# Half products for w_res in the last three blocks, and a changed order of rows, in an attention and gated feed-forward kernel

## The chip, the cores and the metric

The kernel runs on one core of one Trainium2 chip. The metric is the device time of one execution in microseconds. A core has TensorE (PE in the profile; its weight loads are PEld), VectorE (DVE), ScalarE (ACT), GpSimd (POOL) and SyncE (SP), which run side by side, each through its own queue of instructions in order, and wait for each other through semaphores. TensorE writes to PSUM, which has eight banks; VectorE and ScalarE read and write PSUM and SBUF, GpSimd SBUF alone.

## What is computed

Eight batches, eight heads, 576 tokens, head size 64. Without a softmax, attention is two products and a normalisation; its result, seen as 4608 tokens of 512 channels, goes through a gated feed-forward layer with a gated residual:

```python
kv  = einsum('bhsd,bhse->bhde', k, v)
out = einsum('bhsd,bhde->bhse', q, kv)
x   = out / sqrt(mean(out * out) + 1e-6) * g_norm     # as [4608, 512]
ffn = (gelu(x @ w_gate) * (x @ w_val)) @ w_out        # 512 -> 1536 -> 512
y   = x + sigmoid(x @ w_res) * ffn                    # w_res is 512 x 512
```

## The kernel before, in words

**Blocks.** The tokens are worked in nine blocks of 512 (blk 0 to B, B = 8): the first 512 tokens of each batch are a block, and the remaining 64 of each batch make up the last one. TensorE does the matmuls of a block in this order: gate and value products, w_res product, w_out product. The attention of a later batch is laid between them, two blocks ahead. Matmuls have f16 operands of 128x128 (stationary) by 256 or 512 columns and gather in f32 in PSUM.

**Seven products for eight.** From block 2 on most products are made in the manner of Strassen and Winograd: both operands are split into quadrants, sums and differences of quadrants are made beforehand, and seven half-sized products take the place of eight. `gv_group` (L708) does so for four column tiles of w_gate (g) and w_val (v): each half product is four matmuls of 256 columns, named in the order lists (L703) as `1g 1v Eg 5g Ev 5v dg 6g ...`. A digit is a product; `E` is a copy by ScalarE of product 1 out of bank A into bank E, on which product 2 adds; `d` is a copy by ScalarE of product 5 into SBUF; `F` and `c` are sums A + d on VectorE, F back into a PSUM bank, c into SBUF; `g11` to `g22` are the gelu of a quarter on ScalarE; `h11` to `h22` multiply it by the value quarter into the tile `hid`, h22 on GpSimd, the rest on VectorE. Products 6, 7 and 4 add onto the same bank A in turn, so 6 waits for the copies of 1, 7 for the F sum, and 4 for the c sum. A block of three groups takes bank A from two banks by turns, and exchanges the banks of E and F from group to group (`banks_of`, L1263).

**Sums.** `token_sums` (L688) makes four sums of quadrants of a block's transposed tokens, used for w_gate and w_val; `weight_sums` (L662) those of the weights, once. For w_out, `wo_sums` (L465) makes those of the weights, and `s_begin`, `s_rest`, `s_last` (L470 to L482) those of `hid` (s2; s0 and s1; s3), all on VectorE.

**w_res.** `m_res` (L412) does the w_res product in full: for each of four rows of 128 tokens, four matmuls of 512 columns into a bank of its own, then a tanh on ScalarE into `th_all`; 16 matmuls of 512 columns in a block. `m_sigmoid` (L427) makes the sigmoid from the tanh, later.

**w_out.** `out_by_products` (L497) returns four steps: `res(0)`, `res(1)`, `first_two` and `others`. `first_two` makes s3, product wA with its copy to wE, product wD with its copy wd, and the sigmoids; `others` makes the other five products of 12 matmuls each, the sums wF and c22, and the multiplies `pf` by the sigmoid into `osb` (`res_all`). Then `fin` adds x on GpSimd, and `store` issues a store on SP. `out_last` (L577) does this for block 8 in finer steps: u = sigmoid times wd plus x, on GpSimd, spares a later addition, and four pairs of stores go out, on SP's and ScalarE's queues.

**Other work laid between.** `a_t` (L330) writes normalised attention rows t out of PSUM (VectorE, t(0) to t(3), and t(4) for the remaining tokens), `a_x` (L353) multiplies them by g_norm (VectorE), `a_norm` is a chain of twelve small steps on GpSimd. The order of all of this is written out by hand: `at` puts work behind a slot of a block, `at_word(blk, i, word, ...)` behind a word of a group's order list, and `aside_out(blk, key, ...)` ahead of a step of `first_two` and `others` ("D", "F", "00", "22", "01", "11").

Of the kernel before, what the change touches and what calls it, by code (L numbers as in the profile page):

```python
# [18 lines left out]
def kernel(  # L19
# [15 lines left out]
    nc = tc.nc  # L35
# [439 lines left out]
    def s_rest(blk):  # L475
# [2 lines left out]
        sub(nc.vector, s_[0], a_of(blk, 2, 1), a_of(blk, 2, 2), ALU.add)  # L478
        sub(nc.vector, s_[1], s_[0], a_of(blk, 1, 1))

    def s_last(blk):
        sub(nc.vector, hid_sums[3], a_of(blk, 1, 2), hid_sums[1])  # L482

    def prod(ps, a, b, start, es=(0, 1)):

        for e in es:
            for f in range(NFH):
# [6 lines left out]
                    skip_group_check=True,  # L494
                )

    def out_by_products(blk, later, banks, amid):  # L497
        w = {}
        s_ = hid_sums

        def aside(ahead_of):
            for f in amid.get(ahead_of, ()):
                f()

        def res(jj):
            for j in (2 * jj, 2 * jj + 1):
                m_res(blk, j, banks[j])

        def first_two():
            for n in ("D", "E", "F", "A"):  # L510
                w[n] = pmoe.tile([P, 2, CH], FP32, name="w" + n, bank=banks[n])
            w["d"] = attnp.tile([P, 2, CH], FP32, tag="sq", bufs=3, name="wd")
            s_last(blk)
            prod(w["A"], a_of(blk, 1, 1), b_of(1, 1), True)
            nc.scalar.copy(out=w["E"], in_=w["A"])
            aside("D")
            prod(w["D"], s_[0], wo_t[:, 0], True)
            nc.scalar.copy(out=w["d"], in_=w["D"])
            aside("gates")
            for j in range(NJ):  # L520
                m_sigmoid(j)

        def part(jj):
            return slice(None), slice(2 * jj[0], 2 * jj[0] + 2), slice(jj[1] * CH, (jj[1] + 1) * CH)

        def pf(jj, src, eng=nc.vector):
            eng.tensor_tensor(out=res_all[part(jj)], in0=th_all[part(jj)], in1=src, op=ALU.mult)  # L527

        def fin(jj):
            of = part(jj)  # L530
            nc.gpsimd.tensor_tensor(out=res_all[of], in0=res_all[of], in1=t_t[blk][of], op=ALU.add)  # L531

        def store(jj):
            dst = out[blk * S : blk * S + M0, :].rearrange("(p j) c -> p j c", j=NJ)
            js = slice(2 * jj, 2 * jj + 2)
            nc.sync.dma_start(out=dst[:, js, :], in_=res_all[:, js, :])

        def others():


            prod(w["A"], s_[1], wo_t[:, 1], False)
            aside("F")
            sub(nc.vector, w["F"], w["A"], w["d"], ALU.add)
            aside("00")
            prod(w["E"], a_of(blk, 1, 2), b_of(2, 1), False)
            pf((0, 0), w["E"])
            aside("22")
            prod(w["A"], s_[2], wo_t[:, 2], False)
            c22 = res_all[part((1, 1))]
            sub(nc.vector, c22, w["A"], w["d"], ALU.add)  # L550
            aside("01")
            prod(w["F"], s_[3], b_of(2, 2), False)
            pf((0, 1), w["F"])
            aside("11")
            prod(w["A"], a_of(blk, 2, 2), wo_t[:, 3], False)
            if whole(blk + 1):
                pf((1, 1), c22, nc.gpsimd)
                pf((1, 0), w["A"])
            else:
                pf((1, 1), c22)  # L560
                pf((1, 0), w["A"])
            if later:
                return
            for i in (1, 0):
                fin((i, i))
                fin((i, 1 - i))
                store(i)

        if later:
            x = [lambda j=j: a_x(blk, j) for j in range(NJ)]  # L570
            at_word(blk + 1, 0, "1v", *x[0:2], lambda: fin((0, 0)), lambda: fin((0, 1)), lambda: store(0))
            at_word(blk + 1, 0, "Fv", x[2])
            at_word(blk + 1, 0, "cv", x[3])
            at_word(blk + 1, 0, "h22", lambda: fin((1, 0)), lambda: fin((1, 1)), lambda: store(1))
        return [lambda: res(0), lambda: res(1), first_two, others]

    def out_last(blk, banks):  # L577

        s_ = hid_sums

        def bank(n, i):
            return pmoe.tile([P, n, CH], FP32, name="w", bank=i)

        def part(j, n, ch):
            return slice(None), slice(j, j + n), slice(ch * CH, (ch + 1) * CH)

        def gated(j, n, ch, src):
            of = part(j, n, ch)
            nc.vector.tensor_tensor(out=res_all[of], in0=th_all[of], in1=src, op=ALU.mult)

        def plus(j, n, ch, eng):
            of = part(j, n, ch)
            eng.tensor_tensor(out=res_all[of], in0=res_all[of], in1=t_t[blk][of], op=ALU.add)

        def store(j, n, c0, c1):
            for e, queue in enumerate((nc.sync, nc.scalar)):
                dst = out.rearrange("(j e s) c -> e s j c", e=2, s=S)[e, M0:S, j : j + n, c0:c1]
                queue.dma_start(out=dst, in_=res_all[e * R : (e + 1) * R, j : j + n, c0:c1])

        def run():  # L600
            wa = [bank(1, banks["A"][e]) for e in range(2)]
            wd, we, wf = [bank(2, banks[n]) for n in "DEF"]
            d = attnp.tile([P, 2, CH], FP32, tag="sq", bufs=3, name="wd")
            u = attnp.tile([P, 2, CH], FP32, tag="sq", bufs=3, name="u")
            one = (slice(0, 1), slice(1, 2))
            s_last(blk)
            for e in range(2):
                prod(wa[e], a_of(blk, 1, 1), b_of(1, 1), True, (e,))
            for j in (2, 3):
                m_sigmoid(j)  # L610
            for e in range(2):
                nc.scalar.copy(out=we[:, one[e], :], in_=wa[e])
            prod(wd, s_[0], wo_t[:, 0], True)
            nc.scalar.copy(out=d, in_=wd)
            for j in (0, 1):
                m_sigmoid(j)
            for e in range(2):
                prod(wa[e], s_[1], wo_t[:, 1], False, (e,))
                sub(nc.vector, wf[:, one[e], :], wa[e], d[:, one[e], :], ALU.add)
            sub(nc.gpsimd, u, th_all[part(2, 2, 1)], d, ALU.mult)  # L620
            sub(nc.gpsimd, u, u, t_t[blk][part(2, 2, 1)], ALU.add)
            prod(we, a_of(blk, 1, 2), b_of(2, 1), False)
            gated(0, 2, 0, we)
            plus(0, 2, 0, nc.gpsimd)
            store(0, 2, 0, CH)
            prod(wf, s_[3], b_of(2, 2), False)
            gated(0, 2, 1, wf)
            plus(0, 2, 1, nc.gpsimd)
            store(0, 2, CH, C)
            for e in range(2):  # L630
                prod(wa[e], s_[2], wo_t[:, 2], False, (e,))
                gated(2 + e, 1, 1, wa[e])
            of = part(2, 2, 1)
            sub(nc.vector, res_all[of], res_all[of], u, ALU.add)
            store(2, 2, CH, C)
            for e in range(2):
                prod(wa[e], a_of(blk, 2, 2), wo_t[:, 3], False, (e,))
                gated(2 + e, 1, 0, wa[e])
                plus(2 + e, 1, 0, nc.vector)
            store(2, 2, 0, CH)  # L640

        return [lambda: [m_res(blk, j, banks[j]) for j in range(NJ)], run]

    LAST = (B - 1, B)
    GF = 4
# [533 lines left out]
    def plan_attn_ahead(b):  # L1179
# [40 lines left out]
        if whole(m + 1):  # L1220
            t = [lambda j=j: a_t(b, j) for j in range(NJ + 1)]
            x = [lambda j=j: a_x(b, j) for j in range(NJ + 1)]
            for i, word, fs in (
                (0, "Fv", t[2:3]),
                (0, "cv", t[3:4]),
                (1, "1v", x[0:1]),
                (1, "Fv", t[4:5]),
                (1, "cv", x[1:2]),
                (2, "1v", [*x[2:4], lambda: d_xT(b, 0, NJ)]),
                (2, "Fv", [x[4], lambda: d_xT(b, NJ, NJ + 1)]),  # L1230
            ):
                at_word(m + 1, i, word, *fs)
# [21 lines left out]
    for blk in GROUPS:  # L1254
        t = token_sums(blk, nc.vector)
        if blk == 2:
            at(blk - 1, NF + 3, *t)
            continue
        for key, f in zip(("00", "00", "22", "01") if whole(blk) else ("00", "22", "01", "11"), t):
            aside_out(blk - 1, key, f)  # L1260
    out_at = {}

    def banks_of(blk):  # L1263
# [18 lines left out]
        if blk not in LAST:  # L1282
            if len(groups) % 2:
                ga0, ga1, va0, va1, ge_, gf, ve, vf = ga1, ga0, va1, va0, gf, ge_, vf, ve
            out_at[blk] = {0: ge_, 1: ga1, 2: ve, 3: ge_, "A": va1, "D": ga1, "E": ve, "F": ge_}
            att_at[blk] = [gf, vf, ga0, va0]
            pmoe.turn = [out_at[blk][n] for n in "DEFA"]
        else:
            out_at[blk] = {0: ga1, 1: va1, 2: ge_, 3: ve}
# [9 lines left out]
    for blk in range(B + 1):  # L1299
# [21 lines left out]
        else:  # L1321
            slots = [lambda f=f: m_gval(blk, f) for f in range(NF)]
            groups = GROUPS.get(blk, ())
            if groups:
                n = NF - GF * len(groups)
                slots[n:] = [None] * (NF - n)
                ends = []
                at_word(blk, len(groups) - 1, "h12", lambda: s_begin(blk))

                def group(i, blk=blk, ends=ends):  # L1330
                    if i == 0:
# [20 lines left out]
                plan.setdefault(NFH + 2, []).insert(0, lambda: s_begin(blk))  # L1352

            def products(blk=blk, outs=outs):
                s_rest(blk)
                if blk not in GROUPS:
                    out_at[blk] = banks_behind()
                if blk < B:
# [57 lines left out]
```

## Time and profile before

| | |
|---|---|
| Runs of the kernel before | 325.02, 325.13, 324.98, 324.41 us; median 325.0 |
| The profiled execution | 325.02 us; its span, first to last instruction, 323.2 us |
| TensorE (PE) busy | 315.0 us, 97% of the span, 2936 matmuls |
| VectorE (DVE) busy | 263.9 us, 82%, 482 instructions |
| ScalarE (ACT) busy | 201.3 us, 62%, 367 instructions |
| GpSimd (POOL) busy | 145.0 us, 45%, 212 instructions |
| TensorE's mean granted clock | 0.996 of full speed |
| w_res products of blocks 6, 7, 8 start at | 243.04, 274.00, 304.96 us |

How to read it: times in the timelines count from the span's start. A timeline row has the start, the time from the first start to the last end, the engine, the line, the operation, output and inputs with shapes, and how many instructions are merged; in brackets stand the idle time ahead of it and the engine that a program inferred to have ended it. Matmuls overlap: four of 256 columns show 0.60 us from the start of the first to the end of the last, and the next four start 0.437 us after them. Spans on GpSimd are rough. Names in rows are those of the tiles: `Ag` is bank A of the gate product, `wA` that of the w_out product, `rps` the w_res product, `ts` token sums, `hid_s` the sums s0 to s3, `osb` the output rows.

### The profile page before, as it was taken

The page shows a single profiled execution, that of the slowest core. Times are in us where ns is not written, and L with a number is a line of the kernel's source. Part 1 is how long each engine was busy: PE and PEld are TensorE (multiplying, and loading weights), DVE is VectorE, ACT ScalarE, POOL GpSimd, SP SyncE. Part 2 cuts the span into 40 slices and gives each one's busy share as a digit, 9 for nine tenths or more (in the row PEclk, how much of TensorE's full clock was granted, in tenths as well). Part 3 has the DMA queues.
Part 4 walks back from the last instruction along what each step waited for, and adds up shares of the span by engine and source line. Part 5 has one row for each costly group of instructions (what it writes and reads, how often), then busy time and mean ns, then how long its engine had stood idle before and what let it go on. Part 6 is the DMA issues. An engine that isn't in the chain of part 4 may idle for free.

```text
span 323.2 us, 7458 instructions
## 1 busy us (share of the span) xinstructions
PE 315.0 (97%) x2936; PEld 236.4 (73%) x2936; DVE 263.9 (82%) x482; ACT 201.3 (62%) x367; POOL 145.0 (45%) x212
## 2 busy tenths in 40 slices
PE   8989999999999999999999999999999999999993
PEld 3544755444867878886888688868887888788782
DVE  5788879789799887998799879998896777677754
ACT  3673685465727784868487848684766467636760
POOL 2793251573712678337843784117511242042232
PEclk9999999999999999999999999999999999999998
DMA  7999999699995599389938893720322030002004
GB/s 255 324 204 204 194 206 177 164 179 134 156 138 98 180 131 99 133 162 121 112 132 157 109 128 131 118 50 2 130 43 40 2 130 4 0 32 102 0 2 130
DMA packets 76693, 38.89 MB, mean 120 GB/s; under 512 B 42098, under 2 KB 74354, under 8 KB 76658
## 3 DMA queue, kind: packets, MB, share of 16 engines
q0 software_dynamic: 38752, 17.17, 42.1%
q1 hardware_dynamic: 37328, 20.71, 24.9%
q10 hardware_dynamic: 578, 0.52, 0.5%
q8 instruction: 23, 0.38, 0.5%
q14 instruction: 12, 0.10, 0.1%
HBM read 38.80 MB, written 9.44 MB: 149 GB/s over the span
## 4 chain that ended last, share of the span: by engine, by line
PE 96%; DVE 3%; issue 0%; DVEq 0%
PE Av L737 12%; PE Ag L737 12%; PE wA L488 11%; PE rps L415 10%; PE gps L395 6%; PE vps L395 6%; PE Fv L737 6%; PE Fg L737 6%; PE fps L432 3%; PE wD L488 3%; PE Ev L737 3%; PE wF L488 3%; PE wE L488 3%; PE Eg L737 3%; PE w L488 2%; PE idle L902 2%
## 5 line engine op out<-in xcount | busy, mean ns | idle before, releaser
L774 POOL TENSOR_TENSOR hid<-ge,c 128x512 f16<-128x512 f16 x21 | 24.4, 1163 | 69.5 <-ACT ge L768 69.5
L531 POOL TENSOR_TENSOR osb<-osb,t 128x512 f32<-128x512 f32 x28 | 31.6, 1158 | 36.1 <-DVE osb L527 25.1
L488 PEld LDWEIGHTS <-hid_s 128*128 128x128 f16 x384 | 37.5, 98 | 4.4
L737 PEld LDWEIGHTS <-wsv 128*128 128x128 f16 x336 | 32.7, 97 | 4.5
L737 PEld LDWEIGHTS <-wsg 128*128 128x128 f16 x336 | 32.7, 98 | 3.9
L415 PE MATMUL rps<-wr,xT 128*128 128x512 f16 x144 | 33.4, 380 | 0.0
L488 PEld LDWEIGHTS <-hid 128*128 128x128 f16 x288 | 28.1, 98 | 5.1
L747 ACT COPY Eg<-Ag 128x512 f32<-128x512 f32 x21 | 12.2, 582 | 25.9 <-PE Ag L737 25.9
L758 DVE TENSOR_TENSOR Fg<-Ag,d 128x512 f32<-128x512 f32 x21 | 14.6, 697 | 16.4 <-ACT d L751 11.1
L383 ACT ACTIVATE ge<-gps 128x512 f16<-128x512 f32 x24 | 14.1, 597 | 21.3 <-PE gps L395 21.2
L737 PEld LDWEIGHTS <-wg 128*128 128x128 f16 x252 | 24.3, 98 | 3.7 <-issue 0.4
L737 PEld LDWEIGHTS <-wv 128*128 128x128 f16 x252 | 24.6, 97 | 3.3 <-issue 0.2
L424 ACT ACTIVATE th<-rps 128x512 f32<-128x512 f32 x36 | 21.1, 594 | 8.1 <-PE rps L415 8.0
L737 PE MATMUL Ag<-ts,wsg 128*128 128x256 f16 x168 | 25.2, 273 | 0.0
L737 PE MATMUL Av<-ts,wsv 128*128 128x256 f16 x168 | 25.2, 272 | 0.0
L254 DVE TENSOR_REDUCE ss<-sq 128x8 f32<-128x512 f32 x32 | 20.1, 679 | 5.7 <-ACT sq L249 5.7
L415 PEld LDWEIGHTS <-xT 128*128 128x128 f16 x144 | 13.5, 98 | 14.2
L395 PE MATMUL gps<-xT,wg 128*128 128x512 f16 x88 | 22.6, 379 | 0.0
L395 PE MATMUL vps<-xT,wv 128*128 128x512 f16 x88 | 22.6, 379 | 0.0
L488 PE MATMUL wA<-wo_ts,hid_s 128*128 128x256 f16 x168 | 20.6, 273 | 0.0
L384 DVE TENSOR_TENSOR hid<-ge,vps 128x512 f16<-128x512 f16 x24 | 16.3, 685 | 4.8 <-PE vps L395 4.0
L429 ACT ACTIVATE th<-th 128x512 f32<-128x512 f32 x36 | 20.1, 641 | 0.0
(188 smaller groups left out, 766.4 us busy)
## 6 DMA issues: line engine op xcount, KB each, us to landing
out_dram<-osb SPq DMA_DIRECT2D x14, 512.0 KB, 2.6
qraw<-in_q_dram POOLq DMA_DIRECT2D x7, 512.0 KB, 6.9
k<-in_k_dram POOLq DMA_DIRECT2D x7, 512.0 KB, 9.4
v<-in_v_dram POOLq DMA_DIRECT2D x7, 512.0 KB, 11.2
wg<-in_moe_w_gate_dram POOLq DMA_DIRECT2D x2, 512.0 KB, 8.1
wv<-in_moe_w_val_dram POOLq DMA_DIRECT2D x2, 512.0 KB, 8.5
wo<-in_moe_w_out_dram POOLq DMA_DIRECT2D x2, 512.0 KB, 13.9
out_dram<-osb SPq DMA_DIRECT2D x4, 256.0 KB, 4.6
```

Source lines behind the costliest of these rows:

```text
L254: nc.vector.tensor_reduce(out=out_, in_=sqs.pop((b, i)), op=ALU.add, axis=mybir.AxisListType.X)
L383: nc.scalar.activation(out=ge, in_=gps, func=AF.Gelu)
L384: nc.vector.tensor_tensor(out=hids[blk][:, f, :], in0=ge, in1=vps, op=ALU.mult)
L395: nc.tensor.matmul(ps[:, j0 * P : j1 * P], lhsT=w[:, cc, :], rhs=xT_t[blk][:, j0:j1, cc, :], start=(cc == 0 and j0 == 0), stop=(cc == NP - ...
L415: nc.tensor.matmul(rps, lhsT=xT_t[blk][:, j, cc, :], rhs=wr16[:, cc, :], start=(cc == 0), stop=(cc == NP - 1),)
L424: nc.scalar.activation(out=th, in_=rps, func=AF.Tanh, scale=0.5)
L429: nc.scalar.activation(out=th, in_=th, func=AF.Copy, scale=0.5, bias=0.5)
L488: nc.tensor.matmul(ps[:, e - es[0], :], lhsT=a[:, f, e * P : (e + 1) * P], rhs=b[:, f, :], start=(start and e == es[0] and f == 0), stop=( ...
L531: nc.gpsimd.tensor_tensor(out=res_all[of], in0=res_all[of], in1=t_t[blk][of], op=ALU.add)
L737: nc.tensor.matmul(out_[:, r, :], lhsT=lhsT, rhs=rhs, start=(first and r == 0 and c == 0), stop=(c == 1), skip_group_check=True,)
L758: nc.vector.tensor_tensor(out=dst, in0=ps["A", u], in1=sb["d", u], op=ALU.add)
L774: eng.tensor_tensor(out=dst, in0=ge[q], in1=source(q, "v"), op=ALU.mult)
```

## The change

For blocks 6, 7 and 8 (`res_in_halves`), the w_res product is made in seven half products too (`res_halves`): 28 matmuls of 256 columns. Its seven products stand in the order `1 sE 5 sd 6 +F 2 tE 7 +c 3 tF 4 tc tA`, where `s` are copies on ScalarE, `+` sums on VectorE, and `t` the four tanh. Between them are laid the two halves of w_out's product wA (after `sd` and `+F`), the first half of product wD (after `tF`), the sums s0 to s3 one by one (`s_sum`), and the copy to wE. `s_begin`, `s_rest` and `s_last` are left out in these blocks. The wd copy and all four sigmoids follow the last half of wD; in block 8 two of the sigmoids stood ahead of it before. In block 6 the banks of w_res and w_out are given anew.

Four sums of w_res quadrants (`wr_sums`) are made once on VectorE: two in block 5's w_out part, ahead of wD and ahead of the wF sum, two in the last group of block 6, behind `Fv` (ahead of the a_x there) and behind `cv`.

In the first group of blocks 3 to 6, t(2) moves from behind `Fv` to behind `1v`, t(3) from behind `cv` to behind `Fv`. In block 2, two additions `fin` and a store move from behind `1v` to behind `cv` in the recorded order.

```diff
+    def s_sum(blk, i):
+        s_ = hid_sums
+        if i == 0:
+            sub(nc.vector, s_[0], a_of(blk, 2, 1), a_of(blk, 2, 2), ALU.add)
+        elif i == 1:
+            sub(nc.vector, s_[1], s_[0], a_of(blk, 1, 1))
+        elif i == 2:
+            sub(nc.vector, s_[2], a_of(blk, 1, 1), a_of(blk, 2, 1))
+        else:
+            sub(nc.vector, s_[3], a_of(blk, 1, 2), s_[1])
...
+    def res_halves(blk, banks, amid):
...
+        def product(p):
+            n = {1: "A", 2: "E", 3: "F", 4: "A", 5: "F", 6: "A", 7: "A"}[p]
+            first = p in (1, 5)
+            out_ = bank(n) if first else ps[n]
+            s_of = {3: 3, 5: 0, 6: 1, 7: 2}
+            t_of = {4: 3, 5: 0, 6: 1, 7: 2}
...
+            w_ = wr_s[0][:, s_of[p]] if p in s_of else wr_quadrant(*quad[p])
+            x_ = x_sums[blk][:, t_of[p]] if p in t_of else x_quadrant(blk, *xq[p])
+            for e in range(2):
+                for cc in range(2):
+                    nc.tensor.matmul(out_[:, e, :], lhsT=x_[:, e, cc, :], rhs=w_[:, cc, :], ...
...
+        for word in "1 sE 5 sd 6 +F 2 tE 7 +c 3 tF 4 tc tA".split():
+            n = word[-1]
+            if word.isdigit():
+                product(int(word))
+            elif word == "sE":
+                nc.scalar.copy(out=bank("E"), in_=ps["A"])
+            elif word == "sd":
+                sb["d"] = attnp.tile([P, 2, CH], FP32, tag="sq", bufs=3, name="rd")
+                nc.scalar.copy(out=sb["d"], in_=ps["F"])
+            elif word[0] == "+":
+                if n == "c":
+                    sb["c"] = attnp.tile([P, 2, CH], FP32, tag="o32", bufs=3, name="rc")
+                nc.vector.tensor_tensor(out=bank("F") if n == "F" else sb["c"], in0=ps["A"], in1=sb["d"], op=ALU.add)
+            else:
+                tanh(n)
+            for f in amid.get(word, ()):
+                f()
...
+        def with_res():
+            res_halves(blk, dict(zip("AFE", (banks[j] for j in range(3)))), {
+                "sd": [tiles_of_w, lambda: half("A", 0, a_of(blk, 1, 1), b_of(1, 1)), lambda: s_sum(blk, 0)],
+                "+F": [lambda: half("A", 1, a_of(blk, 1, 1), b_of(1, 1)), lambda: s_sum(blk, 1),
+                       lambda: nc.scalar.copy(out=w["E"], in_=w["A"])],
+                "+c": [lambda: s_sum(blk, 2), lambda: s_sum(blk, 3)],
+                "tF": [lambda: half_d(0)],
+            })
+            half_d(1)
+            nc.scalar.copy(out=w["d"], in_=w["D"])
+            for j in range(NJ):
+                m_sigmoid(j)
...
-            at_word(blk + 1, 0, "1v", *x[0:2], lambda: fin((0, 0)), lambda: fin((0, 1)), lambda: store(0))
+            at_word(blk + 1, 0, "1v", *x[0:2])
             at_word(blk + 1, 0, "Fv", x[2])
-            at_word(blk + 1, 0, "cv", x[3])
+            at_word(blk + 1, 0, "cv", x[3], lambda: fin((0, 0)), lambda: fin((0, 1)), lambda: store(0))
...
+        if res_in_halves(blk):
+            return [with_res, lambda: None, lambda: None, others]
         return [lambda: res(0), lambda: res(1), first_two, others]
...
+            half_d(1)
             nc.scalar.copy(out=d, in_=wd)
-            for j in (0, 1):
+            for j in (2, 3, 0, 1):
                 m_sigmoid(j)
...
-                (0, "Fv", t[2:3]),
-                (0, "cv", t[3:4]),
+                (0, "1v", t[2:3]),
+                (0, "Fv", t[3:4]),
...
+    wr_ = wr_sums(nc.vector)
+    aside_out(LAST[0] - 2, "D", wr_[0])
+    aside_out(LAST[0] - 2, "F", wr_[1])
+    for word, f in (("Fv", wr_[2]), ("cv", wr_[3])):
+        at_word(LAST[0] - 1, 2, word, f)
...
             att_at[blk] = [gf, vf, ga0, va0]
+            if res_in_halves(blk):
+                out_at[blk] = {0: ga0, 1: va0, 2: ve, "A": gf, "D": vf, "E": ge_, "F": ga1}
+                att_at[blk] = [ga0, va0, ve, va1]
```

## The prediction

> **What bounds the kernel now.** I read first the page's engine table and its chain that ended last, then the chain in order of time, then each engine's timeline around the edits. The chain is TensorE nearly alone:
>
> ```profile
> PE 96%; DVE 3%; issue 0%; DVEq 0%
> ```
>
> So time is won by fewer matmul columns, or where TensorE waits for a helper; work elsewhere costs only when it makes TensorE or the last store late. In the chain in order of time, block 6 shows both prices (start, us, engine, output, line, count):
>
> ```profile
> 243.20 3.45 PE rps L415 x16
> 246.65 1.31 PE wA L488 x12
> ```
>
> A 512-column matmul takes 3.45/16 = 0.216 us, a 256-column one 1.31/12 = 0.109 us, half: nothing is lost by cutting.
>
> TensorE's timeline gives the waits: a product of four such matmuls starts 0.437 us after the last one where nothing is late, its result is there 0.60 after its start. Block 3, second group:
>
> ```profile
> 133.45 0.60 PE L737 MATMUL Ag<-ts,wsg 128*128 128x256 f16 x4
> 133.99 0.60 PE L737 MATMUL Av<-ts,wsv 128*128 128x256 f16 x4
> ...
> 135.30 0.60 PE L737 MATMUL Ag<-ts,wsg 128*128 128x256 f16 x4
> 135.83 0.60 PE L737 MATMUL Av<-ts,wsv 128*128 128x256 f16 x4
> ```
>
> Both gaps are 0.10 too long (one more of 0.04 stands before 137.61): 0.24 in this group. Its rows on VectorE and ScalarE say why:
>
> ```profile
> 131.13 0.68 DVE L341 TENSOR_TENSOR t<-op,ny 128x512 f16<-128x512 f32 x1
> 131.73 0.68 DVE L774 TENSOR_TENSOR hid<-ge,Ev 128x512 f16<-128x512 f16 x1
> 132.32 0.68 DVE L774 TENSOR_TENSOR hid<-ge,Fv 128x512 f16<-128x512 f16 x1
> ```
> ```profile
> 132.44 0.59 ACT L747 COPY Eg<-Ag 128x512 f32<-128x512 f32 x1
> 133.37 0.57 ACT L747 COPY Ev<-Av 128x512 f32<-128x512 f32 x1 [0.34 <-PE Fg L737]
> ```
>
> The copy to Ev writes the bank that hid<-ge,Fv has read until 133.00 (the releaser named is a guess); it ends 133.94, and the matmuls of 133.99 follow. Block 5 repeats this (Fv read until 198.92, Ev at 199.28, gaps 0.10, 0.09, 0.04). In blocks 4 and 6 Ev starts 0.09 after the read, and the group has no gap.
>
> **The change part by part.** Latencies from the same rows: TensorE's end to VectorE 0.11 (250.58 to 250.69), to ScalarE 0.04; VectorE to TensorE 0.06 (240.80 to 240.86), to ScalarE 0.09.
>
> *Order of t, blocks 3 to 6.* The first t goes ahead of the Fg sum, into 1.20 us in which VectorE sat idle (126.94 to 128.13): free. The second takes the first one's slot, so the hid multiplies come 0.60 earlier; hid<-ge,Fv ends 132.40, Ev follows Eg at 132.96 and ends 133.53, before 133.89. The a_x behind them ends 134.06 as before, since GpSimd's multiply (132.62 to 133.78) holds it. Fg then waits for the matmuls only (133.45 + 0.60 + 0.11 = 134.16, was 134.48), and the gaps of 0.10, 0.09 and 0.04 close. Two blocks: **-0.47**. Ends: 0, if something else than the read held Ev, and -0.48.
>
> *Block 2.* The additions fin((0, 0)) and fin((0, 1)) move in the text, but in the built programs every engine has the same instructions in the same order in block 2, and the additions wait for the same second a_x. The wait they cause stays:
>
> ```profile
> 100.78 2.27 POOL L531 TENSOR_TENSOR osb<-osb,t 128x512 f32<-128x512 f32 x2 [10.61 <-DVE t L355]
> ```
> ```profile
> 99.28 1.42 DVE L355 TENSOR_TENSOR t<-t,g 128x512 f16<-128x512 f16 x4
> ...
> 102.06 1.27 DVE L355 TENSOR_TENSOR t<-t,g 128x512 f16<-128x512 f16 x1
> ```
>
> One a_x took 1.27 instead of 0.41: it could end only 0.28 after GpSimd's addition did. TensorE lost 0.34 + 0.16 there, and will again: **0**.
>
> *Sums of w_res.* Four operations of 128x512 f16, 0.42 us each as the token sums. The first, in block 5, falls into 0.60 us of idle VectorE ahead of 218.09. The second starts 219.29, before the wF sum (219.62, becomes 219.63), and holds GpSimd's first norm step (219.46) some 0.10; the next step waits for a token sum until about 220.5 anyway, which takes the delay up. **0**; at most +0.24, the whole of it, because norm, t (224.10), osb (225.31), Ev (226.07 to 226.64) and the matmuls at 226.77 follow each other closely.
>
> The other two stand in block 6's last group:
>
> ```profile
> 240.72 0.41 DVE L355 TENSOR_TENSOR t<-t,g 128x512 f16<-128x512 f16 x1
> 241.06 0.67 DVE L758 TENSOR_TENSOR c<-Ag,d 128x512 f32<-128x512 f32 x1
> 241.66 0.67 DVE L758 TENSOR_TENSOR c<-Av,d 128x512 f32<-128x512 f32 x1
> ```
>
> One more operation at 240.72 (0.34 apart) moves the c sums to 241.40 and 242.00. 4g (242.16) needs the first at 242.07 + 0.06: in time. 4v (242.60) needs the second at 242.67 + 0.06 = 242.73: **+0.13**. The other sum, behind the c sums, and the later gelu move hid<-ge,Fv from 242.91 to 243.53, end 244.21.
>
> *Half products of w_res.* Per block 28 x 0.109 = 3.06 instead of 3.45: -0.39 each. Waits that come new, counted from the first half product, block 7 (274.00 in the old clock): product 1 at 0, 5 at 0.44, half of wA 0.87, 6 at 1.53, half of wA 1.97, 2 at 2.62, 7 at 3.06, 3 at 3.50, half of wD 3.94, 4 at 4.59, half of wD 5.03, done 5.68 (6.07 before). Product 6 needs the seed of E: 0.64 to 1.22, in time. Product 7 needs the F sum: 6 is there 2.13, sum 2.24 to 2.93 (0.69 as the Fg sum), + 0.06 = 2.99, **0.07 ahead**. On VectorE stand before it hid<-ge,Av (0.56 to 1.24) and s0 (1.16 to 2.11, which needs GpSimd's multiply, 0.69). s1 follows (2.84 to 3.80), then c, 3.77 to 4.46; product 4 needs 4.52, again 0.07 ahead. s2 and s3 end by 6.2; s3's product starts 9.6. The gates: wd copy 5.88, four sigmoids until 8.55; osb<-th,wE waited for them before too and goes with them. Block 7: **-0.39**; ends -0.39 and +0.03 (both loops 0.28 longer, the spread between Ev's 0.09 and 0.36).
>
> Block 6: the E seed goes to the bank that hid<-ge,Fv reads until 244.21, so it runs 244.30 to 244.88; product 6 would start 243.17 + 1.53 = 244.70 and starts 244.94: +0.24. -0.39 + 0.13 + 0.24 = **-0.02**; ends -0.39 and +0.26 (seed 0.28 later).
>
> Block 8: matmuls -0.39 too, but the tail hangs on GpSimd. The sigmoids of rows 2, 3 ran before the wd copy; now all follow it.
>
> ```profile
> 311.90 1.27 POOL L463 TENSOR_TENSOR u<-th,wd 128x512 f32<-128x512 f32 x1 [6.25 <-ACT wd L614]
> 313.25 1.16 POOL L463 TENSOR_TENSOR u<-u,t 128x512 f32<-128x512 f32 x1
> 314.68 2.41 POOL L593 TENSOR_TENSOR osb<-osb,t 128x512 f32<-128x512 f32 x2 [0.28 <-DVE osb L589]
> ```
> ```profile
> 317.00 0.69 DVE L463 TENSOR_TENSOR osb<-osb,u 128x512 f32<-128x512 f32 x1
> ```
>
> The wd copy starts 310.84, the second sigmoid behind it ends 312.45: u starts 312.5 (was 311.90), and the four GpSimd steps end 317.26 (was 317.09). VectorE's osb<-osb,u is ready 0.40 earlier, 316.60, and has two inputs in SBUF like the a_x of block 2. If GpSimd holds it likewise, until 317.13, it ends 317.81 (was 317.69), and the last addition and the last store are 0.12 late: **+0.12**. If not, the last addition ends 318.88 (was 319.28), but the second and third stores now leave 0.2 later, the transfers of the fourth queue behind them, and -0.19 is left. I take +0.12: the a_x row is the nearest, and osb is no less an SBUF operand for being f32. Ends: -0.39 and +0.20.
>
> Sum: -0.47 + 0 + 0 - 0.02 - 0.39 + 0.12 = -0.76. The profiled execution took 325.02 us (span 323.2 and 1.8 around it; the median of four is 325.0): **324.3**. All low ends: -0.48 - 3 x 0.39 = -1.65, 323.4. All high ends: 0 + 0.24 + 0.03 + 0.26 + 0.20 = +0.73, 325.8.
>
> Two rules of the Trainium skill bear on this. The page "TensorE: Matmul & The Clock Gate" (Back-to-back issue gap) gives some 131 ns for 512 columns and 81 for 128 in a sustained stream; an estimate between them for 256 is 98, so 28 x 0.098 = 2.74 against 16 x 0.131 = 2.10 us: halves would cost 0.64 a block, and the sum would be +2.3 instead of -0.76. It speaks against the change; this trace's 216 and 109 ns decide otherwise. "SBUF — State Buffer" (Who interferes with whom) says that a VectorE instruction with two SBUF inputs and a GpSimd one that reads SBUF exclude each other, and names no type; the trace shows it for f16 alone, and by the rule the tail is +0.12.
>
> **The rivals.**
> 1. *The tail is not held* (0.25): a f32 operation is no f16 one, and 317.00 began just as GpSimd ended, so no row shows it. Block 8 gives -0.19: -1.07, 323.95; with block 6's seed unheld too, 323.7.
> 2. *Ev was not held by the read* (0.20): it started 0.36 behind it in blocks 3 and 5 against 0.09 in 4 and 6, so 0.27 has another cause. If that stays on the path, -0.29 is left: 324.7. Against it: started earlier, the 0.27 would run under Eg's copy.
> 3. *Slower: VectorE's sum becomes the bound of the half products* (0.12). Between product 6 and 7, and 7 and 4, the loop of 0.16 + 0.11 + 0.69 + 0.06 = 1.02 has 0.655 + 0.437 = 1.09 of cover; the gate and value groups give the same loop 1.31. A sum that takes 1.27, as the held a_x did, costs 0.51 in each of six loops, +3.1: 327.3. It turns the sign of the sum from 0.07 + 0.76/6 = 0.20 more per loop, and reads slower from 0.30. Against it: GpSimd rests there, and these rows vary by 0.02.
> 4. *Block 2's part works after all* (0.03): -0.50 more, 323.8. The built order speaks against it.
>
> **How the numbers follow.** The forecast has 0.40, its own range 324.0 to 324.5. A measurement tells some 0.2% (0.65 us) from no change, so faster begins at 324.35: 0.28 of the 0.40 and rivals 1 and 4, 0.56. Same: 0.12 and rival 2, 0.32. Slower: rival 3, 0.12. The range 323.5 to 325.0 reaches over rivals 1, 2 and 4.
>
> **What would show it.** rA, rE, rF and wA, wD halves 0.109 apart, from first to last 5.68 in block 7; no gap in the second group of blocks 3 and 5, one of 0.5 still in block 2; in block 6 gaps of 0.13 ahead of 4v and 0.24 ahead of product 6; osb<-osb,u of the tail longer than 0.69. A gap ahead of products 7 or 4 over 0.1 makes the forecast wrong, as does Ev in block 3 still starting 0.9 behind Eg.

## The result, and the profile after

The kernel after takes 323.97 us (median of 52 runs, 323.64 to 326.33), the kernel before 324.55 (74 runs, 324.26 to 326.36). The ratio is 0.9983, with a 95% interval of 0.9977 to 0.9989: 0.55 us faster, between 0.36 and 0.75. That is clear of no change, but less than the 0.2% (0.65 us) from which the prediction speaks of faster: of its three answers, faster (0.56), same (0.32) and slower (0.12), the second came. Predicted were 324.3, with a range of 323.5 to 325.0.

Two executions cannot be compared by their spans alone here. Most executions of either kernel fall into two groups some 0.6 us apart, and in the traces the difference is made in the first 18 us, where TensorE's products wait for loads and their conversions. In the profiled execution of before the first product kvp starts at 9.05 us and the second vps at 18.14; in that of the first experiment below, whose opening has the same instructions, they start at 8.69 and 17.36, and from there to block 2 it stays 0.78 ahead. The profiled execution of before (325.02) is one of the late group, that of after (323.64) one of the early group. So all times below count from one row behind the opening, the first product Fg<-ts,wsg of block 2, at 99.28 us before and 98.53 after:

| us from that row to | before | after | difference | forecast |
|---|---|---|---|---|
| w_res of block 6 | 143.76 | 143.45 | -0.31 | -0.34 |
| w_res of block 7 | 174.72 | 174.24 | -0.48 | -0.49 |
| w_res of block 8 | 205.68 | 204.80 | -0.88 | -0.88 |
| end of the last addition | 220.00 | 219.25 | -0.75 | -0.76 |
| end of the span | 223.96 | 223.33 | -0.63 | -0.76 |

The first line of the chain that ended last, in the page of after:

```profile
PE 92%; DVE 3%; DMA 2%; SPq 1%; POOL 0%; issue 0%; ACT 0%; DVEq 0%; ACTq 0%
```

It is still TensorE's; the DMA share is new since this execution's chain reaches back to a load of the opening.

**Block 3**, second group. TensorE's timeline of after (start, us to the last end, output and inputs, count), of the same products as before:

```profile
132.70 0.60 PE L862 MATMUL Ag<-ts,wsg 128*128 128x256 f16 x4
133.13 0.60 PE L862 MATMUL Av<-ts,wsv 128*128 128x256 f16 x4
...
134.44 0.60 PE L862 MATMUL Ag<-ts,wsg 128*128 128x256 f16 x4
134.88 0.60 PE L862 MATMUL Av<-ts,wsv 128*128 128x256 f16 x4
```

The starts are 0.43 and 0.44 apart, where they were 0.54 and 0.53: the gaps are gone, in block 5 too. VectorE and ScalarE there:

```profile
130.97 0.68 DVE L899 TENSOR_TENSOR hid<-ge,Fv 128x512 f16<-128x512 f16 x1
```
```profile
131.69 0.59 ACT L872 COPY Eg<-Ag 128x512 f32<-128x512 f32 x1
132.20 0.56 ACT L872 COPY Ev<-Av 128x512 f32<-128x512 f32 x1
```

The read of Ev's bank ends at 131.65, before Eg starts, and Ev follows Eg by 0.51 instead of 0.93.

**Block 2.** GpSimd's additions and the a_x that stands beside them are as before (1.27 us; it takes 0.41 elsewhere), and so are the gaps on TensorE, 0.34 and 0.15:

```profile
100.03 2.27 POOL L640 TENSOR_TENSOR osb<-osb,t 128x512 f32<-128x512 f32 x2 [10.61 <-DVE t L355]
```
```profile
101.31 1.27 DVE L355 TENSOR_TENSOR t<-t,g 128x512 f16<-128x512 f16 x1
```
```profile
102.46 0.60 PE L862 MATMUL Fv<-xT,wsv 128*128 128x256 f16 x4
103.24 0.60 PE L862 MATMUL Ag<-ts,wg 128*128 128x256 f16 x4 [0.18 <-DVE c L883]
```

**Block 6.** The chain in order of time leaves TensorE here, for 2.5 us:

```profile
240.72 0.45 PE Fv L862 x4
241.18 0.04 DVEq L899
241.21 0.28 DVE c L883
241.49 0.33 DVE wrs L463
241.83 0.38 DVE hid L899
242.21 0.14 issue
242.35 0.68 DVE hid L899
...
243.11 0.58 ACT rE L568
243.69 0.04 issue
243.73 0.60 PE rA L548 x4
```

Read from below: product 6 (rA, 243.73) waits for the copy rE, that for the second hid (hid<-ge,Fv), which stands behind wrs, the fourth sum of w_res, and the c sums. TensorE's rows show two gaps: 0.11 ahead of 4v (starts 241.00 and 241.55) and 0.22 ahead of product 6.

**Block 7.** Half products, TensorE:

```profile
272.77 0.60 PE L548 MATMUL rA<-wr,xT 128*128 128x256 f16 x4
...
275.39 0.60 PE L548 MATMUL rE<-wr,xT 128*128 128x256 f16 x4
275.82 0.60 PE L548 MATMUL rA<-wrs,ts 128*128 128x256 f16 x4
276.26 0.60 PE L548 MATMUL rF<-wrs,xT 128*128 128x256 f16 x4
276.70 0.82 PE L500 MATMUL wD<-wo_ts,hid_s 128*128 128x256 f16 x6
277.35 0.60 PE L548 MATMUL rA<-wr,ts 128*128 128x256 f16 x4
...
278.44 0.82 PE L500 MATMUL wA<-wo_ts,hid_s 128*128 128x256 f16 x6
```

Product 7 (275.82) and product 4 (277.35) start without a gap, 0.43 behind product 2 and 0.65 behind half of wD; from first to last it is 5.67 us (forecast 5.68).

**Block 8**, the tail. The chain in order of time:

```profile
308.96 5.47 PE w L500 x50
314.43 0.02 issue
314.45 0.43 DVE osb L700
...
314.98 1.23 DVE osb L463
316.21 0.34 DVE osb L700
```

The step of 1.23 is osb<-osb,u, 0.69 before. GpSimd's two additions stand beside it:

```profile
313.39 2.27 POOL L704 TENSOR_TENSOR osb<-osb,t 128x512 f32<-128x512 f32 x2
```

They end at 315.66, and osb<-osb,u, begun at 314.98, at 316.21. In the kernel before it began just as they ended.

### The profile page after: what moved, and what is told of

Read it like the earlier page. It is cut to its first block, busy times and chain, and to the rows that moved or that the text cites. A ratio compares the mean times of both kernels' runs of the same rounds, so it can differ in the third digit from the quotient of the medians.

```text
span 321.9 us, 7558 instructions
## 1 busy us (share of the span) xinstructions
PE 313.1 (97%) x2972; PEld 239.4 (74%) x2972; DVE 271.7 (84%) x492; ACT 203.8 (63%) x373; POOL 144.8 (45%) x212
## 4 chain that ended last, share of the span: by engine, by line
PE 92%; DVE 3%; DMA 2%; SPq 1%; POOL 0%; issue 0%; ACT 0%; DVEq 0%; ACTq 0%
PE Ag L862 11%; PE Av L862 11%; PE wA L500 11%; PE rps L415 7%; PE gps L395 6%; PE vps L395 6%; PE Fv L862 6%; PE Fg L862 6%; PE fps L432 3%; PE Ev L862 3%; PE wD L500 3%; PE Eg L862 3%; PE wF L500 3%; PE wE L500 3%; PE w L500 2%; PE kvp L208 2%
## 5 line engine op out<-in xcount | busy, mean ns | idle before, releaser
L415 PE MATMUL rps<-wr,xT 128*128 128x512 f16 x96 | 22.6, 380 | 0.0
L355 DVE TENSOR_TENSOR t<-t,g 128x512 f16<-128x512 f16 x36 | 19.7, 576 | 0.0
L893 ACT ACTIVATE ge<-Eg 128x512 f16<-128x512 f32 x21 | 12.5, 597 | 10.5 <-PE Eg L862 10.5
```

The lines of the kernel that those rows point to most:

```text
L355: eng.tensor_tensor(out=t_t[blk][:, jj, :], in0=t_t[blk][:, jj, :], in1=g16, op=ALU.mult)
L415: nc.tensor.matmul(rps, lhsT=xT_t[blk][:, j, cc, :], rhs=wr16[:, cc, :], start=(cc == 0), stop=(cc == NP - 1),)
```

## Experiments

Each is the kernel before or after with one edit. "From the common row" is the table's row.

**The order of t alone**, on the kernel before.

```diff
-                (0, "Fv", t[2:3]),
-                (0, "cv", t[3:4]),
+                (0, "1v", t[2:3]),
+                (0, "Fv", t[3:4]),
```

> The kernel before, with the order of t in blocks 3 to 6 alone. Theory (the copy to Ev in the second group waits until hid<-ge,Fv has read that bank): the gaps of 0.10, 0.09 and 0.04 us in blocks 3 and 5 close, Ev starts within 0.1 of that read or right behind Eg, and the time is 0.42 to 0.47 us lower: 324.1. Rival (the read did not hold Ev): Ev still starts 0.9 behind Eg in blocks 3 and 5, at least half of the gaps stay, and the time is no more than 0.2 lower: 324.35 or above.

323.97 us against 324.55; the ratio, 0.9993 (0.9973 to 1.0012), tells nothing by itself. From the common row to w_res of block 6 it is 143.33 us instead of 143.76, to the last addition 219.56 instead of 220.00: -0.43 and -0.44. The gaps of blocks 3 and 5 are gone, Ev stands 0.51 behind Eg. The theory's number holds; that it names the whole cause does not (see the copies on ScalarE).

**The half products alone**: the kernel after with the two lines put back.

> The kernel after, with t(2) and t(3) where they were before. Theory (the order of t and the half products do not act on each other): gaps of 0.23 in each of blocks 3 and 5 come back, blocks 6 to 8 stay as they are in the kernel after, +0.42 to +0.47: 324.4, which leaves the half products a gain of 0.15 over the kernel before. Rival (half products need the earlier t in block 6): block 6 loses more, 324.6 or above.

324.69 us, ratio to before 0.9999 (0.9990 to 1.0008). The gaps of 0.10, 0.09 and 0.04 are back in blocks 3 and 5; to w_res of block 6 it is 143.87 us, to the last addition 219.68, +0.42 and +0.43 against the kernel after. Block 6's gaps are 0.11 and 0.22, as in the kernel after: the median lies where the rival put it (324.6 or above), but the extra loss in block 6 that it rests on is not in the trace. The two parts do not act on each other, and the half products alone are worth 0.32 at the last addition and nothing that the median tells.

**Block 2: the third a_x ahead of the additions**, on the kernel after.

```diff
-            at_word(blk + 1, 0, "1v", *x[0:2])
-            at_word(blk + 1, 0, "Fv", x[2])
+            at_word(blk + 1, 0, "1v", *x[0:3])
```

> The kernel after, with the third a_x of block 2 straight behind the second, so ahead of GpSimd's additions. Theory (GpSimd's addition held that a_x for 1.27 us, and this made the c sums late): the a_x takes 0.41, both c sums are there before products 4g and 4v need them, the two gaps of 0.34 and 0.15 close: -0.5, 323.5. Rival (something else held it, or another VectorE operation with two SBUF inputs is held in its place): a row of 1.2 us stays in this group and the time stays at 323.9 to 324.0.

323.88 us, ratio to before 0.9972 (0.9961 to 0.9982). VectorE and TensorE:

```profile
98.83 1.76 DVE L355 TENSOR_TENSOR t<-t,g 128x512 f16<-128x512 f16 x5
...
102.09 0.69 DVE L882 TENSOR_TENSOR c<-Ag,d 128x512 f32<-128x512 f32 x1 [0.29 <-PE Ag L861]
```
```profile
102.76 0.60 PE L861 MATMUL Fv<-xT,wsv 128*128 128x256 f16 x4
103.20 0.60 PE L861 MATMUL Ag<-ts,wg 128*128 128x256 f16 x4
```

The fifth a_x now takes its 0.34 like the others, the c sum waits for its product and no longer the product for it, and 4g starts 0.44 behind 3v, where it was 0.78. To the last addition it is 218.77 us, -0.48 against the kernel after. Here the theory is shown: the same operation on the same tile, out of the additions' way. The median of the seven executions (323.20 to 323.99) is near the rival's 323.9 and not the 323.5 forecast, but no row of 1.2 us stands in this group any more; it is the rows that decide.

**The tail by quarters**, on the kernel after.

```diff
+                "tc": [lambda: sigmoid(2, 1), lambda: half_d(1), copy_d],
...
-            half_d(1)
-            nc.scalar.copy(out=d, in_=wd)
-            for j in (2, 3, 0, 1):
-                m_sigmoid(j)
+            for j, ch in ((0, 0), (0, 1), (2, 0)):
+                sigmoid(j, ch)
```

> The kernel after, with the sigmoid of block 8 taken by quarters: the quarter that u reads comes first, then the copy of wd, and only then the last tanh and the other quarters. Theory (GpSimd's late u pushes its two additions under osb<-osb,u, which cannot run beside them): u starts at the end of the wd copy, 1.1 us earlier, the additions are done by 315.1, osb<-osb,u takes 0.7 instead of 1.23, the last addition ends 0.5 earlier and the time is 0.4 to 0.6 lower: 323.5. Rival (the end hangs on the last matmuls and the stores, not on u): osb<-osb,u becomes short, yet the time moves by less than 0.15.

323.04 us, ratio to before 0.9957 (0.9944 to 0.9971). GpSimd's last addition and VectorE's osb<-osb,u:

```profile
314.33 1.15 POOL L704 TENSOR_TENSOR osb<-osb,t 128x512 f32<-128x512 f32 x1 [0.16 <-DVE osb L700]
```
```profile
315.34 0.69 DVE L463 TENSOR_TENSOR osb<-osb,u 128x512 f32<-128x512 f32 x1
```

u starts 310.24, at the end of the wd copy. The additions follow their multiplies and end as osb<-osb,u becomes ready; it takes 0.69. To the last addition it is 218.73 us, -0.52. The rival falls. (The median of five executions is 0.93 below that of the kernel after, more than the 0.4 to 0.6 forecast; the trace gives -0.52 at the last addition and -0.65 at the end of the span.)

**Banks of rE and wE exchanged in block 6**, on the kernel after.

```diff
-                out_at[blk] = {0: ga0, 1: va0, 2: ve, "A": gf, "D": vf, "E": ge_, "F": ga1}
-                att_at[blk] = [ga0, va0, ve, va1]
+                out_at[blk] = {0: ga0, 1: va0, 2: ge_, "A": gf, "D": vf, "E": ve, "F": ga1}
+                att_at[blk] = [ga0, va0, ge_, va1]
```

> The kernel after, with the banks of rE and wE in block 6 exchanged, so that the seed of rE goes to a bank that a gelu has read and not hid<-ge,Fv. No instruction moves. Theory (that read holds the seed, and the seed product 6): rE starts 0.04 behind rA's matmuls, the gap of 0.22 ahead of product 6 closes: -0.22, 323.75. Rival (ScalarE or VectorE is late there anyway): the seed starts at 243.1 in the old clock, and the time stays at 323.9 to 324.0.

323.86 us, ratio to before 0.9975 (0.9963 to 0.9987), beside a before of 324.90 in this set. The seed rE starts 0.09 behind the end of rA's matmuls and product 6 has no gap. But the next product waits:

```profile
245.38 0.60 PE L548 MATMUL rE<-wr,xT 128*128 128x256 f16 x4
245.93 0.60 PE L548 MATMUL rA<-wrs,ts 128*128 128x256 f16 x4
```
```profile
244.32 0.95 DVE L463 TENSOR_TENSOR hid_s<-hid 128x1536 f16<-128x1536 f16 x1
245.19 0.69 DVE L575 TENSOR_TENSOR rF<-rA,rd 128x512 f32<-128x512 f32 x1
```

Product 6's result is there at 244.29 + 0.60 + 0.11 = 245.00, the F sum starts 0.19 later, behind s0, and product 7 is 0.11 late. To w_res of block 7 it is 174.13 us, -0.11 of the 0.22 expected. The bank is shown as what held the seed; half of its gap passes on to VectorE.

**The last two sums of w_res earlier in block 6**, on the kernel after.

```diff
-    for word, f in (("Fv", wr_[2]), ("cv", wr_[3])):
-        at_word(LAST[0] - 1, 2, word, f)
+    for i, f in ((0, wr_[2]), (1, wr_[3])):
+        at_word(LAST[0] - 1, i, "cv", f)
```

> The kernel after, with the last two sums of w_res taken in the first and the second group of block 6, behind cv, not in its last. Theory (the one ahead of the c sums makes product 4v 0.11 late, both make hid<-ge,Fv and through it product 6 0.22 late): both gaps close, -0.33, 323.65; if the sums make hid<-ge,Fv late in the groups where they now stand, up to 0.2 of it comes back as gaps behind Ev there. Rival (the gap of product 6 belongs to the bank and not to the sums): only the gap of 4v closes, -0.11, 323.85.

323.56 us, ratio to before 0.9968 (0.9954 to 0.9983). Both gaps of block 6 are gone, product 6 starting 0.65 behind the half of wA ahead of it, and none comes ahead of product 7 or in the groups that now hold the sums:

```profile
243.58 0.82 PE L500 MATMUL wA<-wo,hid 128*128 128x256 f16 x6
244.23 0.60 PE L548 MATMUL rA<-wrs,ts 128*128 128x256 f16 x4
```

To w_res of block 7 it is 173.92 us, -0.32. So the gap of product 6 needs both, the bank and the sums that make its reader late.

**Less cover between products 6 and 7**, on the kernel after, blocks 6 and 7.

```diff
-                "sd": [tiles_of_w, lambda: half("A", 0, a_of(blk, 1, 1), b_of(1, 1)), lambda: s_sum(blk, 0)],
-                "+F": [lambda: half("A", 1, a_of(blk, 1, 1), b_of(1, 1)), lambda: s_sum(blk, 1),
+                "sd": [tiles_of_w, lambda: half("A", 0, a_of(blk, 1, 1), b_of(1, 1)),
+                       lambda: half("A", 1, a_of(blk, 1, 1), b_of(1, 1)), lambda: s_sum(blk, 0)],
+                "+F": [lambda: s_sum(blk, 1),
```

> The kernel after, with both halves of wA ahead of product 6 in blocks 6 and 7, so that only product 2 (0.437 us) stands between product 6 and product 7. Theory (the loop from product 6 over the F sum to product 7 takes 1.02 us): a gap of 0.58 ahead of product 7 in both blocks; in block 6 the gap of 0.22 ahead of product 6 goes, since it starts 0.655 later: +0.94 in sum, 324.9. Rival (the loop is shorter or starts before product 6 is done, so the cover between the halves was not needed): no gap over 0.2 ahead of product 7, 323.8 to 324.2.

324.79 us, ratio to before 0.9998 (0.9983 to 1.0013). Block 7:

```profile
275.46 0.60 PE L548 MATMUL rA<-wrs,ts 128*128 128x256 f16 x4
275.90 0.60 PE L548 MATMUL rE<-wr,xT 128*128 128x256 f16 x4
276.92 0.60 PE L548 MATMUL rA<-wrs,ts 128*128 128x256 f16 x4 [0.42 <-DVE rF L575]
```

Product 7 starts 1.02 behind product 2, a gap of 0.58, and 1.46 behind product 6; block 6 shows the same gap and none ahead of product 6. To w_res of block 8 it is 205.76 us, +0.95. Counted as in the prediction, from 0.44 behind product 6's start, the loop takes 1.46 - 0.44 = 1.02 us, which is what the prediction had added up.

**Block 8 as before**, on the kernel after (`res_in_halves` true for blocks 6 and 7 only, `out_last` of the kernel before).

> The kernel after, with block 8 as in the kernel before: w_res in full, two sigmoids ahead of the copy of wd. Theory (block 8's half products are paid back in the tail, 0.13 by the last addition and up to 0.25 by the last landing): 0.1 to 0.25 lower, 323.75 to 323.85, with osb<-osb,u at 0.69. Rival (the matmul columns that were saved count): 0.2 to 0.4 higher, 324.2 to 324.4.

323.90 us, ratio to before 0.9977 (0.9963 to 0.9991), which does not tell it from the kernel after. By the trace the last addition ends 219.13 us from the common row, -0.12, with osb<-osb,u at 0.69, and the span 223.06, -0.27. Block 8's half products save 0.39 of matmuls and give back more: the theory holds by the trace, at its upper end.

**Four tiny copies on ScalarE**, on the kernel before. The prediction had left open why Ev starts 0.36 behind the read in blocks 3 and 5, and 0.09 in blocks 4 and 6.

```diff
+    spare = consts.tile([P, 1], FP32, name="spare")
+    at(1, 3, *[lambda: nc.scalar.copy(out=spare, in_=eps_col)] * 4)
```

> The kernel before with four tiny copies more on ScalarE in block 1, nothing else. In the kernel before, the two late Ev copies (blocks 3 and 5) are ScalarE instructions that stand exactly 128 apart in its program, and each began 0.27 later than a copy in blocks 4 and 6 that waits for the same kind of read. Theory A (the 0.27 belongs to the place in ScalarE's program): Ev of blocks 3 and 5 starts 0.09 behind the read of hid<-ge,Fv, their gaps of 0.10, 0.09 and 0.04 close or shrink, up to 0.47 lower, 324.0, and an instruction four places earlier starts some 0.27 late instead. Theory B (the 0.27 belongs to what the blocks do, banks or reads): Ev still starts 0.36 behind the read in blocks 3 and 5, same gaps, 324.4 to 324.6.

324.09 us, ratio 0.9988 (0.9979 to 0.9998). VectorE and ScalarE in block 3:

```profile
131.59 0.68 DVE L774 TENSOR_TENSOR hid<-ge,Fv 128x512 f16<-128x512 f16 x1
```
```profile
132.36 0.57 ACT L747 COPY Ev<-Av 128x512 f32<-128x512 f32 x1
```

The read is as late against its group as before, and still Ev starts 0.09 behind its end (132.27). The gaps of 0.10, 0.09 and 0.04 are gone in both blocks; to the last addition it is 219.55 us, -0.45. Adding four useless instructions gains as much as the order of t. One part of theory A did not come true: no instruction four places earlier starts later than it did. The instructions that now stand at numbers 192 and 320 are gelus with nothing to wait for.

**A hundred and thirty copies**, on the kernel before, spread over blocks 0 and 1: 128 places on, net of two instructions that fall away.

> The kernel before with 130 tiny copies more on ScalarE in blocks 0 and 1, which moves the Ev copies of blocks 3 and 5 by exactly 128 places in ScalarE's program (two other instructions of its program fall away). The copies cost time in blocks 0 to 2, so only the rows of blocks 3 and 5 are read. Theory A (a place that comes again every 128 instructions makes a waiting copy some 0.27 late): both Ev copies start 0.36 behind the read of hid<-ge,Fv again, and the gaps of 0.10, 0.09 and 0.04 are back. Theory B (any added instruction takes them off it, or the four copies changed something else): Ev starts 0.09 behind the read as with four copies, no gaps.

338.1 us, which is the copies' own price. Block 3, VectorE, ScalarE, TensorE:

```profile
145.40 0.68 DVE L774 TENSOR_TENSOR hid<-ge,Fv 128x512 f16<-128x512 f16 x1
```
```profile
146.45 0.57 ACT L747 COPY Ev<-Av 128x512 f32<-128x512 f32 x1 [0.34 <-PE Fg L737]
```
```profile
146.53 0.60 PE L737 MATMUL Ag<-ts,wsg 128*128 128x256 f16 x4
147.07 0.60 PE L737 MATMUL Av<-ts,wsv 128*128 128x256 f16 x4
```

Ev is 0.37 behind the read again, the gap of 0.10 is back, and 0.09 and 0.04 behind it; block 5 repeats it. Theory B falls. Of theory A it stands that these copies are late at these places, not that every waiting instruction is, 128 places on: number 448 of ScalarE's program in the kernel before is a gelu that had waited 0.99 us for the sum c<-Ag,d, and it starts 0.03 after that sum's end (272.09 + 0.69 = 272.78):

```profile
272.81 0.63 ACT L768 ACTIVATE ge<-c 128x512 f16<-128x512 f32 x1 [0.99 <-DVE c L758]
```

**Three edits together**, on the kernel after: block 2, the tail, the earlier sums.

> The kernel after with three of the edits together: the third a_x of block 2 ahead of GpSimd's additions, the tail of block 8 by quarters, the last two sums of w_res in the first two groups of block 6. Theory (three separate stalls on TensorE and at the end, none of which uncovers another): 0.50 + 0.33 + 0.53 = 1.36 lower than the kernel after: 322.3 against executions whose opening is alike, a ratio to the kernel before of 0.994. Rival (one stall gone makes the next one show, as the exchanged banks did ahead of product 7): 322.7 or above.

322.37 us against 324.45, ratio 0.9943 (0.9925 to 0.9962): faster than both kernels. To the last addition it is 217.86 us, -1.39 against the kernel after. The forecast was -1.36; at the last addition the three edits alone gave -0.48, -0.52 and -0.30. No new stall shows.

## Why the prediction was right, and where not

**The starting point.** The forecast of -0.76 was taken off an execution of 325.02, one with late first loads; the median of more runs is 324.55. That explains that 323.97 lies below 324.3 although the gain was smaller than forecast. The two errors partly cancel in the time, which is luck. At the end of the last addition the sum was right (-0.75); the trace's span gives -0.63, the medians -0.58.

**Order of t, -0.47.** Measured -0.42 to -0.44 in two pairs (the order of t added to the kernel before, and taken out of the kernel after). "The copy to Ev writes the bank that hid<-ge,Fv has read" is one half of the cause. Rival 2 said that 0.27 of the 0.36 has another cause, and that was right: it comes and goes with the place of Ev in ScalarE's program. Its price was wrong, since it supposed that the 0.27 stays on the path. With the earlier read Ev does not wait at all, and the 0.27 does not appear. The gap needs a late read and that place; either edit removes it.

**Block 2, 0.** As forecast. The third a_x alone was the cause, and the 0.5 could be had by moving it.

**w_res, blocks 6 and 7.** Gaps of 0.11 and 0.22 in block 6 (forecast 0.13 and 0.24) and none in block 7: -0.06 and -0.40 for -0.02 and -0.39. The half products start 0.437 us after each other where nothing is late, 109 ns for each matmul, and a full product's 16 matmuls take 3.45, 216 ns each. The Trainium skill, page "TensorE: Matmul & The Clock Gate" (Back-to-back issue gap), gives 131 ns for 512 columns in a sustained stream and would have made the half products a loss; these runs differ from it, and the measured -0.40 decides. The low end of -0.39 for block 6 was too generous: with the seed on time, VectorE's s0 holds the F sum, so 0.11 of the 0.22 passes on.

**Rival 3.** Its loop is shown to be 1.02 us, and its cover of 1.09 was needed: less cover cost 0.58 a block. It did not come because no row of the loop grew (F sum 0.70, c sum 0.68 in block 7).

**Block 8, +0.12.** This is the term that was mis-sized. At the last addition it is +0.13, by the mechanism that was forecast: osb<-osb,u took 1.23 us and ended 0.55 behind GpSimd's addition. The prediction took the end of the last addition for the end. From there to the end of the span it is 3.96 us before and 4.07 after; in the six profiled kernels whose osb<-osb,u was held it is 4.05 to 4.14, in the seven others 3.93 to 3.96. So the hold goes with 0.1 to 0.2 more in the last stores, and block 8 comes to +0.25 by the end of the span, above the term's own high end of +0.20. The rows show where it lies: counted from the end of the last addition, the first pair of stores is issued 3.21 us ahead of it in the six and 3.41 in the seven, the last pair at the same 0.03 behind it, and the last store lands 2.95 to 3.05 behind it instead of 2.84 to 2.87. That the stores, now closer together, hold each other up fits this but was not tested. The 0.11 was just enough to bring the gain below the 0.65 that the prediction called faster: its chance for that, 0.28 of the forecast's 0.40, had only 0.11 us between -0.76 and the bound.

## What to carry to other kernels

Cheaper products move the bound to what stands beside them: of 3 x 0.39 us of matmuls saved, 0.33 went to two stalls in block 6 and all of block 8's to a GpSimd step that a later sigmoid had pushed under a VectorE step. When VectorE and GpSimd both work on operands in SBUF, look at which step of one begins inside a step of the other, and move it out of there; two such moves gave 1.0 us, more than the change itself. And where a change is worth less than the scatter of the opening, count from a row behind it.

## What the runs showed of the hardware

- A ScalarE copy that waits for a semaphore started some 0.27 us late at two places 128 instructions apart in ScalarE's program (numbers 192 and 320 before and with the half products alone; 320 and 448 with 130 copies more), and not four places off, nor where it had nothing to wait for. The place alone is not enough: the gelu at number 448 before, which had waited 0.99 us, was not late. What happens at these places was not settled. A clue is that an 8 KB transfer of instructions (DMA queue q14) begins 0.65 to 0.69 us after the start of each of the six late copies (147.14 and 213.03 us with 130 copies), and with four copies more ahead of the same Ev copies, at 130.95 and 196.66.
- A VectorE operation with two f32 operands in SBUF does not run beside GpSimd's f32 addition: 1.23 us instead of 0.69 in all six profiled kernels where it began inside one, 0.69 in the seven where it began in the last 0.15 us of one. The Trainium skill's page "SBUF — State Buffer" (Who interferes with whom) states the exclusion without a type; these runs agree, for f32 as for f16, and add the price: the held operation ended 0.55 behind GpSimd's.
